# The order of the symmetry checks on VectorE: half comparisons spread between row comparisons, and W's loads behind the second row instead of the third

## The chip, the cores and the metric

The kernel runs on one core of one Trainium2 chip. The metric is the time of one execution on the device, in microseconds. It is in float32, and one launch computes everything.

## The reference

One FNet layer with a pre-norm is followed by one mixture-of-depths layer with a capacity of one token. The input `x` has 2048 tokens of 576 values.

```python
h  = x + FNet(layernorm(x))          # FNet: real part of a 2-D DFT
#   a = z @ dft_hid_re.T,  b = z @ dft_hid_im.T       (z = layernorm(x))
#   y = dft_seq_re @ a - dft_seq_im @ b               (2048 x 2048 matrices)
h2 = h + MoD(layernorm(h))
#   r = z2 @ w_r ; the token with the largest r goes through
#   (silu(z2 @ w_gate) * (z2 @ w_up)) @ w_down, times sigmoid(r)
#   (w_gate, w_up: 576 x 4608, w_down: 4608 x 576); all other tokens get nothing
```

All five matrices of the layers are inputs, so the DFT matrices too have to be read, and the kernel may not assume what they contain.

## The kernel before

**Folding.** A DFT matrix is symmetric under reversal of its index: the cosine is even, the sine odd. The kernel uses that to do only a part of the multiplications. Because the matrices are inputs, it also reads them from HBM in full and compares on the chip what it did not multiply with, against what it did. If any comparison differs, a flag (`miss`) decides at the end what is stored.

**Tiling.** Tokens are laid out as 128 partitions x 16 slots of 576 values (`X`). Column tiles of the sequence matrices are numbered j = 0..15, with part i = 0 (cosine) or 1 (sine); one such tile, "(j,i)", is 128 x 1152 float32 (576 KB by the profile's DMA issues) for the rows that are used, and a mirror part of 128 x 896 that is read only to be compared. The tiles come in two groups, `GROUPS = [[1,2,3,4,5],[6,7,0,8]]`. Those of group one (index 0 in the code) stay in the buffer `D` for the matmuls, their counterparts 16−j and all mirrors pass through the raw buffers `R` and through the free places of `D`.

**The comparisons.** There are two kinds.

- A row comparison, `c_check(j, i)`, makes three passes on VectorE: mirror of (j,i) against (j,i), mirror of (16−j,i) against (16−j,i) (both 896 wide, `off_s`, recorded as L418 or L420), and (16−j,i) against (j,i) (1152 wide, `off_t`, also L418 or L420). L418 is the form that also writes an accumulator. The call also loads what is missing: (16−j,i) on SP's queue (L394) and the mirrors by a gather on GpSimd's queue (L333).
- A half comparison, `c_half(g, c, m)`, compares the two halves of m tiles of `D`, in both parts, in passes of 128 x 5 x 64 and 128 x 4 x 64 per tile (`off_h`, L449 on VectorE; L423 is a short pause between two passes). For group one there are three: tiles 0–1, tiles 2–3, tile 4 (`HALVES[0] = [(0,2),(2,2),(4,1)]`). It loads nothing.

Each comparison writes its differences in bfloat16 to one of two slots of `Q`; ScalarE squares and sums them (L405), and the slot is free again after that. So each comparison waits for the square of the one two before it.

**W.** `w_first` issues the loads of the hidden-DFT matrix on SP's queue (L465 twice, 576 KB each, and a small one, L467), `wc_first` one gather of it on GpSimd's queue (L333 into `W`). W is needed by the hidden matmuls (L686) and by its own comparisons (`w_check`, `wc_check`).

**Queues.** SP issues plain loads in program order: a load whose buffer isn't free holds all loads behind it. GpSimd issues the gathers in its own program order, between its arithmetic. The profile lists the two as q1 and q0.

**The order.** A planner (`Plan.add`, `Plan.order`) gets all operations with an estimated duration and dependences, and lays out each engine's sequence. `Q` slots, raw buffers and the queues' order are assigned in the order in which the code calls the functions above, so the order of these calls sets which comparison comes after which, and which load is ahead of which. Between the comparisons VectorE also has the folds of the sequence results (`keep_step`, L659 into `Z`), the residuals (L695) and the router's dots (L699).

**The end.** The weights of the expert (L1330, L1338) are loaded by SP after the DFT matrices. VectorE, GpSimd (L1358) and ScalarE (L1363) form the products with the token, TensorE the last one (L1384); the last row is finished at L1395 and stored at L1405.

Of the kernel before, what the change touches and what calls it, by code (L numbers as in the profile page):

```python
# [37 lines left out]
GROUPS = [[1, 2, 3, 4, 5], [6, 7, 0, 8]]  # L38
# [5 lines left out]
HALVES = [[(0, 2), (2, 2), (4, 1)], [(0, 2), (2, 2)]]  # L44
# [31 lines left out]
class Plan:  # L76
# [6 lines left out]
    def add(self, eng, dur, fn, *deps, tail=0.0, push=0.0, holds=False, moves=False):  # L83
        flat = []
        for d in deps:
            flat += d if isinstance(d, list) else [d]
        n = {"eng": eng, "dur": dur, "fn": fn, "deps": [d for d in flat if d], "tail": tail, "push": push}
        n["holds"], n["moves"] = holds, moves
        n["i"] = len(self.ops)
        self.ops.append(n)  # L90
        return n
# [72 lines left out]
def kernel(  # L164
# [272 lines left out]
    def half_on_pool(g, c, i):  # L437
        return g == 1
# [343 lines left out]
    def then(f, *args):  # L782
        return lambda: f(*args)
# [41 lines left out]
    for a, b in X_RUNS:  # L825
# [4 lines left out]
        m = [add("ACT", 0.95, then(measure, k), f, push=push) for k, f in zip(ks, r)]  # L830
# [28 lines left out]
    for k in FOLDED:  # L859
        dg, use, at = [], [], []  # L860
        for sl in slots_of(k):
            n = next(places)
            UF[sl] = LATER[n]
            at.append(PLACE[n])
            if k in PAIRS:
                u, w = dgs.take()
# [42 lines left out]
    def c_load(j, i, mirror):  # L909
        CU[j, i, mirror] = ring("POOL" if mirror else "SP", load_c, 0.46 if mirror else 0.59, j, i, mirror)  # L910

    def c_first(g, i, cs=None):

        for c, j in enumerate(GROUPS[g]):
            if cs is not None and c not in cs:
                continue
            u = D_TAG[g, i], c
            if u in free:
                free.remove(u)
            w, users[u] = users[u], []  # L920
            LAST["SP"], d = load("SP", then(load_c, None, j, i, False), 0.59, w, LAST["SP"])
            CU[j, i, False] = u, d

    def c_half(g, c, m):
        u, w = qs.take()
        cus = [[CU[j, i, False] for j in GROUPS[g][c : c + m]] for i in range(2)]
        n = [
            add(
                *(("POOL", 0.3 + 1.31 * m) if half_on_pool(g, c, i) else ("DVE", 0.16 + 0.62 * m)),
                then(off_h, g, c, m, i, u), [d for _, d in cus[i]], w, PASSED if half_on_pool(g, c, i) else None,  # L930
                holds=not half_on_pool(g, c, i),
            )
            for i in range(2)
        ]
        for i in range(2):
            for b, _ in cus[i]:
                users[b].append(n[i])
        if (g, c + m) == (1, len(GROUPS[1])):
            HELD.append((u, 9 * m * P, n))
            return  # L940
        squares(u, 9 * m * P, n)
# [5 lines left out]
    def squares(u, w, n, ps=P, behind=None):  # L947
        SQUARES.append(add("ACT", 0.3 + w / 1200, then(square, u, w, ps), n, behind))
        qs.users[u].append(SQUARES[-1])

    def c_check(j, i):

        u, w = qs.take()
        u0, d0 = CU[j, i, False]
        c_load(j, i, True)
        u1, d1 = CU[j, i, True]
        n = [add("DVE", 1.08, then(off_s, j, i, u, 0), d0, d1, w, holds=True)]
        if (j, i) == GATE:
            PASSED.append(add("POOL", 0.1, lambda: pool.tensor_copy(gate[:, 1:2], gate[:, 0:1]), n))
        users[u0] += n  # L960
        users[u1] += n
        free.append(u1)
        if j in PAIRS:
            m = NK - j
            c_load(m, i, False)
            c_load(m, i, True)
            (u2, d2), (u3, d3) = CU[m, i, False], CU[m, i, True]
            n.append(add("DVE", 1.08, then(off_s, m, i, u, 1), d2, d3, w, holds=True))
            users[u3].append(n[1])
            n.append(add("DVE", 1.36, then(off_t, j, i, u), d0, d2, w, holds=True))  # L970
            users[u0].append(n[2])
            users[u2] += n[1:]
            free.extend([u3, u2])
        if u0[0] == "D1":
            free.append(u0)
        squares(u, QW if j in PAIRS else 7 * P, n)
# [3 lines left out]
    def w_first():  # L980
        for n in range(3):
            LAST["SP"], d = load(
                "SP", then(load_w, None, n), (0.59, 0.59, 0.005)[n], LAST["SP"], users["W" + "ABC"[n]]
            )
            WL.append(d)

    def wc_first():
        LAST["POOL"], d = load("POOL", then(load_w, None, 5), 0.295, LAST["POOL"])
        WC.append(d)

    def w_check():
        for n in range(2):
            u, d = ring("POOL", load_w, 0.59, n + 3)
            q, w = qs.take()
            o = add("DVE", 2.2, then(off_w, n, q), WL[n], d, w, holds=True)
            users[u].append(o)
            squares(q, 3 * D, o)
            WS.append(o)
            free.append(u)

    def wc_check():
        q, w = qs.take()
        WS.append(add("DVE", 2.6, then(off_wc, q), WL[2], WC, w))
        squares(q, D + 289, WS[-1])
# [91 lines left out]
        for b in [b for b in free if type(b) is tuple and b[0] == tag]:  # L1096
            free.remove(b)

    for c, m in HALVES[0]:
        c_half(0, c, m)  # L1100
    for n, j in enumerate(GROUPS[0]):
        if n == 3:
            w_first()
        if n == 3:
            wc_first()
        c_check(j, 0)
    for n in (0, 1, 4, 2, 3):
        seq_step(0, n)
        keep_step(0, n)
# [8 lines left out]
    no_more("D2")  # L1118
    free += [("D0", n) for n in range(N_D["D0"])]
    rows, first = iter(GROUPS[0]), iter(range(len(GROUPS[1])))  # L1120
    for step in "sffsffwcsss":
        if step == "s":
            c_check(next(rows), 1)
        elif step == "f":
            c_first(1, 0, (next(first),))
        elif step == "c":
            wc_check()
        else:
            w_check()
# [109 lines left out]
    step = add("DVE", 0.25, T["steps"][0], SCORES)  # L1239
    most = add("PE", 0.4, T["steps"][1], step)  # L1240
    step = add("DVE", 0.45, T["steps"][2], step)
    step = add("PE", 0.4, T["steps"][3], step, most)
    qx = add("DVE", 0.4, from_result, SCORES)
    rows = add("DVE", 0.55, T["steps"][4], most)
    slot = add("DVE", 1.1, token, step, rows)
    step = add("DVE", 1.0, where, slot, qx)
    step = add("ACT", 2.0, row_of_token, step, slot, RESULTS)
    squares(*HELD[0], behind=step)
    near = add("POOL", 1.0, other_rows, slot, push=50.0)
    step = add("PE", 1.2, to_all, step)  # L1250
# [33 lines left out]
    for b in range(NJ // TW):  # L1284
        j = TW * b
# [202 lines left out]
    with tc.If(T["mv"], preferred_fallthrough_block=False):  # L1488
        with ExitStack() as gen:
# [33 lines left out]
            with ExitStack() as hs:  # L1523
# [9 lines left out]
                with tc.For_i(0, NK, 1) as k:  # L1533
                    dve.tensor_copy(xr, row_of(GX, k))
                    norm(xn, xr, "x")
                    for a in range(5):
                        w = min(P, D - a * P)
# [4 lines left out]
                    for c in range(4):  # L1542
                        pa = zbank(f"gpa{c}")
                        for a in range(5):
                            w = min(P, D - a * P)
# [115 lines left out]
```

## Time and profile before

| | before |
|---|---|
| time, median of 3 runs | 197.28 us (195.94 to 198.41) |
| the profiled execution's own time | 197.32 us |
| its span | 195.3 us |
| mean granted TensorE clock | 0.86 |
| VectorE busy | 163.7 us (84%) |
| ScalarE busy | 140.4 us (72%) |
| TensorE busy | 130.8 us (67%) |
| GpSimd busy | 119.3 us (61%) |
| moved by DMA | 77.74 MB, mean 398 GB/s |

The span runs from the first to the last recorded instruction; the execution's own time is 2.0 us longer. Busy shares are means over stages: the checks and the DFT lie between 30 and 125 us, the router around 125 to 150 us, and the expert up to the end. A `DMA` row gives the mean busy share of the 16 DMA engines.

### The profile page before, as it was taken

The numbers are of one execution on the slowest core, as the hardware profiler recorded it, in microseconds if no ns is written. First come the engines' busy times: TensorE is split into PE (matmuls) and PEld (weight loads), VectorE is DVE, ScalarE is ACT, GpSimd is POOL, SyncE is SP. The second block draws the span as 40 slices with busy tenths as digits, with TensorE's granted clock in tenths as the row PEclk, the third lists the DMA queues.
The fourth block names the chain that finished last, engine by engine and source line by source line (L and its number), as shares of the span: only waits on it lengthen the run. The fifth ranks groups of instructions, "written<-read, shape, count | busy, mean of one in ns | idle before, by whom it ended". The sixth has DMA issues, their size and how long they took to land.

```text
span 195.3 us, 2824 instructions
## 1 busy us (share of the span) xinstructions
PE 130.8 (67%) x758; PEld 89.9 (46%) x758; DVE 163.7 (84%) x430; ACT 140.4 (72%) x260; POOL 119.3 (61%) x152
## 2 busy tenths in 40 slices
PE   0007999999999999999699989800241425073960
PEld 0005667765767788677576767500121212030340
DVE  2399999999899999997799999999739999979620
ACT  3298854782898697499289979697679898986600
POOL 6588888761515874076170006968639999999500
PEclk9999999999999999999999999985555555555599
DMA  5999999999999999999999999999999999999992
GB/s 182 414 413 411 412 411 406 411 403 396 408 410 411 413 404 406 408 413 411 407 403 392 422 428 393 422 410 368 425 426 425 416 433 425 421 419 416 411 425 92
DMA packets 14483, 77.74 MB, mean 398 GB/s; under 512 B 1911, under 2 KB 1915, under 8 KB 11134
## 3 DMA queue, kind: packets, MB, share of 16 engines
q1 hardware_dynamic: 10340, 56.34, 71.5%
q0 software_dynamic: 4112, 21.17, 26.8%
q8 instruction: 7, 0.11, 0.2%
q14 instruction: 14, 0.11, 0.2%
q10 hardware_dynamic: 10, 0.00, 0.0%
HBM read 72.78 MB, written 6.49 MB: 406 GB/s over the span
## 4 chain that ended last, share of the span: by engine, by line
DVE 31%; POOL 15%; issue 15%; DMA 11%; PE 5%; ACT 2%; ACTq 0%; SPq 0%; POOLq 0%; DVEq 0%
DVE Q L420 11%; POOL D L1358 8%; DMA R<-in_ct_dram 7%; DVE junk L699 6%; DMA D<-in_wt_dram,iw 4%; DVE X L695 4%; PE pd L1384 3%; DVE Z L659 2%; POOL R L1358 2%; DVE Q L418 2%; PE pk L1392 2%; POOL R L333 1%; POOL W L1358 1%; ACT Q L405 1%; POOL Q L1358 1%
## 5 line engine op out<-in xcount | busy, mean ns | idle before, releaser
L405 ACT ACTIVATE Q<-Q 128x2944 bf16<-128x2944 bf16 (+5 forms) x26 | 54.7, 2104 | 12.7 <-DVE Q L420 7.6
L686 PE MATMUL py<-W,Z 128*128 128x289 f32 x180 | 45.3, 409 | 1.0 <-DVE X L695 1.0
L641 PE MATMUL ps<-D,XF 128*128 128x320 f32 (+3 forms) x216 | 44.9, 407 | 1.6 <-DVE Z L659 1.6
L333 POOL DMA_INDIRECT R<-in_ct_dram,ic x22 | 24.7, 1121 | 27.3 <-DVE Q L420 15.9
L686 PEld LDWEIGHTS py<-W,Z 128*128 128x128 f32 x180 | 33.7, 189 | 12.3 <-PE py L686 1.8
L641 PEld LDWEIGHTS ps<-D,XF 128*128 128x128 f32 (+1 forms) x216 | 32.2, 172 | 13.8 <-issue 3.2
L1358 POOL TENSOR_TENSOR D<-D,Z 128x1152 f32<-128x1152 f32 x7 | 18.3, 2642 | 0.0
L574 ACT ACTIVATE junk<-X,XT 128x576 bf16<-128x576 f32 x16 | 12.3, 771 | 7.5 <-DVE W L535 6.3
L718 ACT ACTIVATE junk<-X,TD 128x576 bf16<-128x576 f32 x16 | 12.3, 768 | 5.4 <-DVE X L695 5.3
L420 DVE TENSOR_TENSOR Q<-D 128x896 bf16<-128x896 f32 (+1 forms) x13 | 15.0, 1186 | 1.0 <-ACT Q L405 1.0
L418 DVE SCALAR_TENSOR_TENSOR Q<-R,D 128x896 bf16<-128x896 f32 (+1 forms) x11 | 13.4, 1216 | 2.9 <-DMA R<-in_ct_dram 2.7
L420 DVE TENSOR_TENSOR Q<-R,D 128x896 bf16<-128x896 f32 (+1 forms) x13 | 15.0, 1163 | 0.0
L613 PE MATMUL fo<-W,diag 128*128 128x288 f32 (+1 forms) x8 | 4.2, 706 | 16.0 <-DVE diag L604 16.0
L333 POOL DMA_INDIRECT D<-in_ct_dram,ic x10 | 11.9, 1189 | 4.0 <-DVE Q L420 1.8
L699 DVE SCALAR_TENSOR_TENSOR junk<-X,wrz 128x576 bf16<-128x576 f32 x16 | 12.0, 752 | 0.4
L748 ACT ACTIVATE X<-X,BB,UP 128x576 f32<-128x576 f32 x14 | 10.9, 852 | 2.0 <-DVE BB L731 2.0
L695 DVE SCALAR_TENSOR_TENSOR X<-py,X 128x576 f32<-128x576 f32 x16 | 11.7, 753 | 0.0
L1384 PE MATMUL pd<-XF,H 128*1 128x144 f32 x80 | 5.1, 406 | 9.8 <-DVE H L1376 6.1
L1363 ACT ACTIVATE junk<-D 128x576 bf16<-128x576 f32 x16 | 10.9, 683 | 0.9 <-POOL D L1358 0.3
L1384 PE MATMUL pd<-D,H 128*1 128x144 f32 x128 | 7.5, 400 | 5.4 <-DVE H L1376 5.4
L447 POOL TENSOR_TENSOR Q<-D 128x640 bf16<-128x640 f32 (+1 forms) x8 | 11.0, 1400 | 0.0
L1347 DVE SCALAR_TENSOR_TENSOR junk<-R,xsp 128x576 bf16<-128x576 f32 x14 | 10.5, 751 | 0.3
(208 smaller groups left out, 264.9 us busy)
## 6 DMA issues: line engine op xcount, KB each, us to landing
D<-in_ct_dram SPq DMA_DIRECT2D x23, 576.0 KB
R<-in_ct_dram SPq DMA_DIRECT2D x9, 576.0 KB
D<-in_wu_dram SPq DMA_DIRECT2D x4, 1152.0 KB
D<-in_wd_dram SPq DMA_DIRECT2D x4, 1152.0 KB
R<-in_wg_dram SPq DMA_DIRECT2D x3, 1152.0 KB
D<-in_wg_dram SPq DMA_DIRECT2D x3, 1152.0 KB
R<-in_wu_dram SPq DMA_DIRECT2D x3, 1152.0 KB
out_dram<-X SPq DMA_DIRECT2D x2, 1440.0 KB
```

The lines of the kernel that those rows point to most:

```text
L333: pool.indirect_dma_start(tile, None, view, bass.IndirectOffsetOnAxis(ap=rows, axis=0), element_offset=at)
L405: act.activation(t, t, AF.Square, accum_out=DS[0 : t.shape[0], n : n + 1])
L418: dve.scalar_tensor_tensor(o, a, 1.0, b, op0=OP.mult, op1=op, accum_out=cell)
L420: dve.tensor_tensor(o, a, b, op=op)
L574: act.activation(junk[:, 0:D], X[:, k, 0:D], AF.Square, bias=XT[:, n : n + 1], scale=-float(D), accum_out=VX[:, n : n + 1],)
L641: pe.matmul(cm(ZP[g, n][k % 2][p0 : p0 + m], w), XF[:, q, m0 : m0 + m], DT[g, i][:, :, k, 0:HM], start=k in (0, 1), stop=k in (6, 7),)
L686: pe.matmul(YP[GROUPS[g][c]][:, h, 0:w], Z[:, a, c * P : (c + 1) * P], w_block(a)[:, h * HD : h * HD + w], start=(a == 0), stop=(a == 4),)
L695: dve.scalar_tensor_tensor(t, y, 1.0, t, op0=OP.mult, op1=OP.add, accum_out=TD[:, n, 1:2])
L699: dve.scalar_tensor_tensor(halves_of(junk2), halves_of(X[:, k, 0:D]), 1.0, YP["w"], op0=OP.mult, op1=OP.mult, accum_out=ON["dot"][:, n : n ...
L718: act.activation(junk[:, 0:D], X[:, k, 0:D], AF.Square, bias=TD[:, n, 1:2], scale=-float(D), accum_out=VAR[:, n : n + 1],)
L1358: pool.tensor_tensor(t, t, xs.unsqueeze(1).to_broadcast([P, JW, D]), op=OP.mult)
L1384: pe.matmul(T["pd"][at(h), :QD], H[:, j : j + 1], WB["d", j0][:, r, h * QD : (h + 1) * QD], start=(j == 0), stop=(j == NJ - 1),)
```

## The change

Before, the three half comparisons of group one are called first, then the rows 1 to 5 of part 0, with W's loads ahead of the fourth row. Now the calls follow the string `hrhrwrrr`: half comparison of tiles 0–1, row 1, half comparison of tiles 2–3, row 2, W's loads (plain and gathered), rows 3, 4 and 5. The third half comparison (tile 4) is called later, in the next string, behind row 1 of part 1 (`shffsffwcsss`).

```diff
-    for c, m in HALVES[0]:
-        c_half(0, c, m)
-    for n, j in enumerate(GROUPS[0]):
-        if n == 3:
+    pairs, rows = iter(HALVES[0]), iter(GROUPS[0])
+    for step in "hrhrwrrr":
+        if step == "h":
+            c_half(0, *next(pairs))
+        elif step == "w":
             w_first()
-        if n == 3:
             wc_first()
-        c_check(j, 0)
+        else:
+            c_check(next(rows), 0)
...
     rows, first = iter(GROUPS[0]), iter(range(len(GROUPS[1])))
-    for step in "sffsffwcsss":
-        if step == "s":
+    for step in "shffsffwcsss":
+        if step == "h":
+            c_half(0, *next(pairs))
+        elif step == "s":
             c_check(next(rows), 1)
         elif step == "f":
             c_first(1, 0, (next(first),))
```

Below the changed lines the line numbers grow by three (L1330 becomes L1333).

The first place is SP's queue, where the ten loads of group one's tiles into `D` end and the loads for the row comparisons into `R` begin; `W` is the hidden-DFT matrix. Before:

```order
L394 DMA D<-in_ct_dram 128x1152 x10
L394 DMA R<-in_ct_dram 128x1152 x3
L465 DMA W<-in_wt_dram 128x2x576 x2
L467 DMA W<-in_wt_dram 2x576
L394 DMA D<-in_ct_dram 128x1152
L394 DMA R<-in_ct_dram 128x1152 x2
L394 DMA D<-in_ct_dram 128x1152 x2
```

And now:

```order
L394 DMA D<-in_ct_dram 128x1152 x10
L394 DMA R<-in_ct_dram 128x1152 x2
L465 DMA W<-in_wt_dram 128x2x576 x2
L467 DMA W<-in_wt_dram 2x576
L394 DMA R<-in_ct_dram 128x1152
L394 DMA D<-in_ct_dram 128x1152
L394 DMA R<-in_ct_dram 128x1152 x2
```

The three loads into `R` are the tiles (15,0), (14,0) and (13,0), for the rows 1, 2 and 3. The third of them now stands behind W's three loads. On GpSimd's queue W's gather moves likewise, from behind two gathers of mirrors to ahead of them.

The second place is VectorE from the first row comparison on (`ps` and `os` are the sequence results that go to `Z`, `bt` belongs to the router). Before, from the first pass of row 1:

```order
L418 SCALAR_TENSOR_TENSOR Q,spill<-R,D 128x896
L418 SCALAR_TENSOR_TENSOR Q,spill<-R,D 128x1152
L420 TENSOR_TENSOR Q<-R 128x896
L659 SCALAR_TENSOR_TENSOR Z<-ps_0_395,os_0_425 128x5x64 x2
L449 TENSOR_TENSOR Q<-D 128x5x64
L423 SCALAR_TENSOR_TENSOR spill<-eps 128x1
L449 TENSOR_TENSOR Q<-D 128x4x64
L449 TENSOR_TENSOR Q<-D 128x5x64
L449 TENSOR_TENSOR Q<-D 128x4x64
L823 TENSOR_SCALAR bt<-tf 128x16
L420 TENSOR_TENSOR Q<-D,R 128x896
L420 TENSOR_TENSOR Q<-R,D 128x1152
```

And now, from the end of the second half comparison, row 1 being ahead of it, to the three passes of row 3:

```order
L449 TENSOR_TENSOR Q<-D 128x2x5x64
L449 TENSOR_TENSOR Q<-D 128x2x4x64
L823 TENSOR_SCALAR bt<-tf 128x16
L420 TENSOR_TENSOR Q<-R,D 128x896
L659 SCALAR_TENSOR_TENSOR Z<-ps_0_392,os_0_427 128x5x64 x2
L418 SCALAR_TENSOR_TENSOR Q,spill<-R,D 128x1152
L420 TENSOR_TENSOR Q<-R 128x896
L659 SCALAR_TENSOR_TENSOR Z<-ps_1_415,os_1_457 128x5x64 x2
L420 TENSOR_TENSOR Q<-R,D 128x1152
L420 TENSOR_TENSOR Q<-D,R 128x896
L420 TENSOR_TENSOR Q<-R,D 128x896
```

The half comparison of tile 4 no longer stands between rows 1 and 2. The rows 2 and 3 follow each other with only the first two folds into `Z` between them, and row 3 now begins with its 1152-wide pass, which reads the tile (13,0).

The third place is VectorE at the first two rows of part 1, ahead of the first residual (L695). Before:

```order
L659 SCALAR_TENSOR_TENSOR Z<-ps_3_492,os_3_522 128x5x64 x2
L418 SCALAR_TENSOR_TENSOR Q,spill<-R,D 128x1152
L418 SCALAR_TENSOR_TENSOR Q,spill<-R,D 128x896
L418 SCALAR_TENSOR_TENSOR Q,spill<-R 128x896
L418 SCALAR_TENSOR_TENSOR Q,spill<-R,D 128x1152
L418 SCALAR_TENSOR_TENSOR Q,spill<-R,D 128x896
L420 TENSOR_TENSOR Q<-R 128x896
L695 SCALAR_TENSOR_TENSOR X,TD<-py_0_532,X 128x576
```

And now:

```order
L420 TENSOR_TENSOR Q<-R 128x896
L659 SCALAR_TENSOR_TENSOR Z<-ps_3_491,os_3_523 128x5x64 x2
L449 TENSOR_TENSOR Q<-D 128x5x64
L423 SCALAR_TENSOR_TENSOR spill<-eps 128x1
L449 TENSOR_TENSOR Q<-D 128x4x64
L449 TENSOR_TENSOR Q<-D 128x5x64
L449 TENSOR_TENSOR Q<-D 128x4x64
L418 SCALAR_TENSOR_TENSOR Q,spill<-R,D 128x1152
L418 SCALAR_TENSOR_TENSOR Q,spill<-R,D 128x896
L420 TENSOR_TENSOR Q<-R 128x896
L695 SCALAR_TENSOR_TENSOR X,TD<-py_0_535,X 128x576
```

The half comparison of tile 4 (four passes and a pause) now stands between the rows 1 and 2 of part 1, and the last fold into `Z` stands between row 1 and it.

## The prediction

> **What bounds the kernel now.** I read the page's DMA rows first, then the chain of waits, then VectorE's timeline and the queues' rows in short windows. The page:
>
> ```profile
> GB/s 182 414 413 411 412 411 406 411 403 396 408 410 411 413 404 406 408 413 411 407 403 392 422 428 393 422 410 368 425 426 425 416 433 425 421 419 416 411 425 92
> DVE 31%; POOL 15%; issue 15%; DMA 11%; PE 5%; ACT 2%; ACTq 0%; SPq 0%; POOLq 0%; DVEq 0%
> ```
>
> The chain names VectorE first, with 31%, and the transfers with only 11%. But the transfer rate hardly falls in any slice. The table of windows (time in each engine, granted clock, then the share of the 16 DMA engines and GB/s) says how full they are:
>
> ```profile
> 5.00:40.00 35.00, 23.65 (x83) 16.97 (x84) 30.50 (x114) 23.80 (x51) 28.60 (x70) 1.00 1.02 411
> 40.00:80.00 40.00, 40.00 (x178) 28.91 (x177) 38.25 (x65) 29.22 (x38) 18.89 (x18) 1.00 1.02 407
> 80.00:86.00 6.00, 5.59 (x23) 4.08 (x22) 6.00 (x13) 4.87 (x7) 2.51 (x2) 1.00 1.01 406
> 86.00:115.00 29.00, 27.38 (x134) 20.64 (x133) 26.26 (x41) 22.94 (x35) 9.51 (x9) 1.00 1.01 409
> 115.00:150.00 35.00, 14.77 (x53) 10.28 (x51) 29.50 (x104) 28.53 (x47) 23.41 (x31) 0.72 1.01 411
> 150.00:190.00 40.00, 19.41 (x292) 9.04 (x292) 31.55 (x90) 29.53 (x83) 33.11 (x13) 0.56 1.01 421
> ```
>
> The DMA share is 1.01 or 1.02 in every stretch from 5 to 190 us. So the 16 DMA engines never lack work, and the kernel ends some microseconds after the last weights have come. The change moves no bytes away. A wait on VectorE is then worth something only if it decides when a load is issued late enough for the queues to run empty; and each microsecond in which they are empty is one at the end. No gain can come from filling them better.
>
> **What of VectorE's time the change can move.** Its timeline, with the wait ahead of an instruction in brackets:
>
> ```profile
> 41.08 0.48 DVE L449 TENSOR_TENSOR Q<-D 128x320 bf16<-128x320 f32 x1
> 42.63 0.17 DVE L823 TENSOR_SCALAR bt<-tf 128x16 f32<-128x16 f32 x1
> 43.24 1.09 DVE L420 TENSOR_TENSOR Q<-D,R 128x896 bf16<-128x896 f32 x1 [0.44 <-ACT Q L405]
> 46.52 0.88 DVE L659 SCALAR_TENSOR_TENSOR Z<-ps,os 128x320 f32<-128x320 f32 x2
> 47.32 1.34 DVE L420 TENSOR_TENSOR Q<-R,D 128x1152 bf16<-128x1152 f32 x1
> 52.55 3.36 DVE L420 TENSOR_TENSOR Q<-D 128x896 bf16<-128x896 f32 x3 [0.95 <-ACT Q L405]
> 59.89 0.88 DVE L659 SCALAR_TENSOR_TENSOR Z<-ps,os 128x320 f32<-128x320 f32 x2
> 60.69 1.35 DVE L418 SCALAR_TENSOR_TENSOR Q<-R,D 128x1152 bf16<-128x1152 f32 x1
> 64.41 1.41 DVE L418 SCALAR_TENSOR_TENSOR Q<-R,D 128x1152 bf16<-128x1152 f32 x1
> 67.88 0.75 DVE L695 SCALAR_TENSOR_TENSOR X<-py,X 128x576 f32<-128x576 f32 x1
> 76.97 3.36 DVE L420 TENSOR_TENSOR Q<-D 128x1152 bf16<-128x1152 f32 x3
> 94.11 1.36 DVE L418 SCALAR_TENSOR_TENSOR Q<-R,D 128x1152 bf16<-128x1152 f32 x1 [2.70 <-DMA R<-in_ct_dram]
> ```
>
> Two waits for ScalarE's squares stand here, 0.44 and 0.95 us, 1.39 together; with the half comparisons spread, both go. They are the most that the new order can save on VectorE.
>
> **W's loads ahead of row 3's.** Row 3 begins with a pass over (13,0), whose load is now behind W's. Up to and including it SP's queue carries the same bytes as before up to W's end. A tile has, by the page,
>
> ```profile
> D<-in_ct_dram SPq DMA_DIRECT2D x23, 576.0 KB
> ```
>
> which is 0.59 MB, half of W as much (128 x 1152 float32 too), and the nine slots of `X` that SP loads half of that each, 9 x 0.295: 2.65 + 10 x 0.59 + 3 x 0.59 + 2 x 0.59 = 11.5 MB. What q1, SP's queue, had moved from the start to 36, 46, 47 and 90 us, one answer each:
>
> ```profile
> q1 hardware_dynamic: 2448, 9.76, 69.6%
> q1 hardware_dynamic: 3085, 11.42, 63.9%
> q1 hardware_dynamic: 3132, 11.55, 63.3%
> q1 hardware_dynamic: 5436, 20.94, 59.1%
> ```
>
> 11.5 MB are through at 46.7 us. That is the lower bound for the landing of (13,0). A load lands later than the count of bytes says, since the 16 engines don't keep step: 20.94 MB is the sum up to the load of the chain's rows below (29 tiles, X and W), reached at 90.0, and that load landed at 80.74 + 13.28 = 94.0, which is 4.0 later. So the upper bound is 50.7 us; I take the middle, 48.7.
>
> When does VectorE ask? Rows 1 and 2 are done earlier now, since only half of the half comparisons stand ahead: before, `Z`'s second fold ended at 46.52 + 0.80 = 47.32. Now 1.55 us of the third half comparison (41.08 to 42.63) and the 0.44 wait are gone from before it, and about 0.9 us come in at row 1: its second pass reads (15,0) at about 35, where it read it at 38 before (bounds 0 and 3, by bytes near 1). So VectorE asks at about 46.2 and stands for 2.5 us, from 0.5 to 4.5, where before the load of (13,0) had come long before W.
>
> **From row 3 to the first residual.** Before, from 47.32 to 67.88, 20.56 us, 0.95 of them the wait. The new order does the same in between plus the half comparison of tile 4, 1.55 us: 21.15 us. Its second row of part 1 needs the slot of the first row, whose square ScalarE takes as that row ends:
>
> ```profile
> 64.35 2.66 ACT L405 ACTIVATE Q<-Q 128x2944 bf16<-128x2944 bf16 x1 [1.59 <-issue]
> 66.91 0.19 ACT L405 ACTIVATION_READ_ACCUMULATOR Q<-Q 128x1 f32 x1
> ```
>
> That is 2.85 us, and between the two rows VectorE has a fold (0.80) and the half comparison (1.55), 2.35: a wait of 0.5, or over 1 if ScalarE still makes the copy for that fold first; I take 0.7. The first residual then comes at 48.7 + 21.15 + 0.7 = 70.55, against 67.88: VectorE is 2.7 us late, from 0.7 (landing at 46.7) to 4.7 (50.7). The removed waits are in this sum.
>
> **Who waits for that.** The order on VectorE from there to the comparisons of row 3, part 1 (76.97, three passes) is the same as before. SP stands behind them, in the chain and in SP's own timeline:
>
> ```profile
> 79.25 1.09 DVE Q L420
> 80.36 0.33 SPq L394
> 80.74 13.28 DMA R<-in_ct_dram
> ```
>
> ```profile
> 72.81 7.87 SPq L394 DMA_DIRECT2D D<-in_ct_dram  x4
> ```
>
> One load goes at 73, the next three and the one into `R` only as these passes end, 79 to 81. What each queue moved in single microseconds, 81:82, then 82:83 (two rows), then 83:84 (two rows):
>
> ```profile
> q0 software_dynamic: 73, 0.41, 102.4%
> q0 software_dynamic: 45, 0.24, 61.6%
> q1 hardware_dynamic: 31, 0.14, 35.5%
> q1 hardware_dynamic: 84, 0.37, 91.0%
> q0 software_dynamic: 13, 0.05, 12.5%
> ```
>
> From 81 to 82 SP's queue moved nothing; GpSimd's gathers in q0 alone kept the engines full. At 82.0 they had 0.24 + 0.05 MB left and a little after, some 0.3 MB or 0.8 us at 0.41 MB/us, so they end at 82.8; SP's data come from about 82.3. The margin is 0.5 us. No gather can step in: GpSimd's next one waits for VectorE too. With VectorE 2.7 us late, SP's data come at 85.0, and the engines are empty from 82.8 to 85.0, for **2.2 us**. Bounds: 0.2 (late by 0.7) and 4.2 (by 4.7).
>
> From there VectorE's own lateness is no second cost: it had 2.70 us to stand at 91.4 for the load issued at 80.74. All later loads shift by the 2.2 us, with an engine share of 1.01 there is nothing in which to catch up, and the end follows.
>
> **The small terms.** W's gather ahead of two gathers of mirrors holds these up by about one gather,
>
> ```profile
> L333 POOL DMA_INDIRECT R<-in_ct_dram,ic x22 | 24.7, 1121 | 27.3 <-DVE Q L420 15.9
> ```
>
> 1.1 us; row 3 waits for (13,0) anyway: nothing. One pause less, 0.08 us, and one pass of row 1 in the cheaper form: in the 0.9 above, nothing. At the end the products have one row against a shift,
>
> ```profile
> 180.82 2.62 POOL L1358 TENSOR_TENSOR R<-R,Z 128x1152 f32<-128x1152 f32 x1 [0.33 <-SPq L1488]
> ```
>
> so GpSimd has 0.33 us to spare there, and the end takes the whole shift.
>
> The sum: 197.3 + 2.2 = **199.5 us**, on the profiled run's own 197.32 (span 195.3 and 2.0 around it), which is also the median, 197.28.
>
> **Two rules of the Trainium skill.** In 36 to 47 us the two queues shared the engines like this:
>
> ```profile
> q0 software_dynamic: 475, 2.61, 60.0%
> q1 hardware_dynamic: 684, 1.79, 42.8%
> ```
>
> The Trainium skill ("DMA: Bandwidth & Descriptors", section "Queues, rings and completion order") says that a DMA engine alternates between the queue rows that have work, a packet of each in turn. By an equal split of time, q1 would reach 11.5 MB about 1.5 us sooner (an estimate from that page and the rows), and the sum would be 198.0; the measured 42.8% decides here. What it says against the change holds either way: W's loads get no more than their turn, while the gathers run, and row 3's load stands behind them.
>
> **The rivals.**
>
> *The queues never run dry.* If (13,0) lands at 46.7, or loads released earlier by rows 1 and 2 leave more in the queues at 82 us, VectorE is late by less than the margin and the 2.70 us at 91.4 take the rest: **197.3**. For it: the full share everywhere. Against it: 0.5 us is a small margin.
>
> *The new order helps.* The 1.39 us of waits go, and loads are issued sooner. The transfers bound this: from 5 to 190 us there is no gap in their share to fill, so at most a few tenths at the ends, **196.9**.
>
> *A fuller queue moves more per microsecond.* As a mechanism: up to 115 us the engines move 409 GB/s with a share of 1.01, later up to 425 in single slices. If loads issued ahead brought the early part to 425, the 45 MB of 5 to 115 us (the first four rows of the windows, stretch by rate) would take 106 instead of 110 us: 197.3 − 4.1 = **193.2**. The rows speak against it: the share is full at either rate. The Trainium skill ("Perfetto Trace Analysis", section "Roofline") puts the ceiling of one core's 16 DMA engines at about 435 GB/s; the rows here stay below it, at 433 at most.
>
> *Slower by over 2%.* The same drought, longer: it is over the bound of 3.95 us once VectorE is over 4.45 us late at the passes of 76.97, which is so if (13,0) lands at 50.5 or later. At the upper bound 50.7 the engines stand for 4.2 us: **201.5**. For it: one load did land 4.0 us after its bytes' count. Against it: rows 1 and 2 free buffers earlier, and the load's lag was measured under a longer queue.
>
> **How the numbers follow.** Two per cent, 3.95 us, is about what a measurement of this kernel can tell from no change; faster is below 193.3, slower above 201.2. Chances: my forecast 0.50 (198.4 to 201.2), dry for longer 0.14, never dry 0.29, a small gain 0.05, the rate that rises 0.02. So faster 0.02, same 0.84, slower 0.14. The range runs from 196.7, which takes in the case without a drought, to 201.5, where the upper bound of the landing ends.
>
> **What would show it.** Right: on VectorE a wait of 1 to 4 us for `R<-in_ct_dram` ahead of a 1152-wide L420 at about 46 us; the brackets `<-ACT Q L405` of 0.44 and 0.95 gone; the first residual at 70 to 71 us; a slice between 80 and 90 us with a DMA share well below 1; the 2.70 us wait still there, or shorter, some 2 us later. Wrong: the first residual at 68.5 or earlier, or a full share from 5 to 190 us again; then the time is that of before. If the drought comes at 53 to 56 us, where row 3's late passes free their buffers, the mechanism is right and the place wrong. I would be wrong on the sign if the span came out below 195 us.

## The result and the profile after

The changed kernel takes 198.56 us (median of 20 runs, 197.51 to 200.43), the one before 196.45 us (median of 20, 195.71 to 198.41): a ratio of 1.0119, 95% interval 1.0098 to 1.0141. It is slower by 1.2%, clear of 1 by its interval, and by less than the 2% up to which the prediction calls the times the same. The forecast was 199.5 against 197.3, a ratio of 1.011. The size came out; the way there, as the trace shows, is another one. One profiled execution below, that of the kernel with fourteen more matmuls, was a disturbed one (204.47 us, that kernel's others 198.95 to 201.38), so that only durations are read from it and it is left out of the last table.

VectorE's timeline of the changed kernel at the places of the forecast:

```profile
46.12 1.36 DVE L420 TENSOR_TENSOR Q<-R,D 128x1152 bf16<-128x1152 f32 x1
64.44 1.36 DVE L418 SCALAR_TENSOR_TENSOR Q<-R,D 128x1152 bf16<-128x1152 f32 x1 [0.90 <-ACT Q L405]
67.87 0.75 DVE L695 SCALAR_TENSOR_TENSOR X<-py,X 128x576 f32<-128x576 f32 x1
76.96 3.36 DVE L420 TENSOR_TENSOR Q<-D 128x1152 bf16<-128x1152 f32 x3
94.46 1.36 DVE L418 SCALAR_TENSOR_TENSOR Q<-R,D 128x1152 bf16<-128x1152 f32 x1 [3.06 <-DMA R<-in_ct_dram]
```

Row 3's pass at 46.12 has no wait in brackets. The first residual comes at 67.87, before at 67.88, and the passes that SP waits for at 76.96, before at 76.97. VectorE is not late at all there, and so the queues don't run dry. The windows:

```profile
80.00:86.00 6.00, 6.00 (x26) 4.63 (x26) 5.96 (x13) 4.87 (x7) 2.65 (x2) 1.00 1.01 405
115.00:150.00 35.00, 20.60 (x68) 14.64 (x66) 25.98 (x94) 25.81 (x44) 20.21 (x29) 0.74 1.00 398
```

The share from 80 to 86 us is 1.01 as before. In the stretch from 115 to 150 us TensorE is busy for 20.6 us instead of 14.8, and VectorE for 26.0 instead of 29.5. There the time goes. The chain of waits of the changed kernel goes through it: VectorE's residuals (L695) at 112.79, TensorE's hidden matmuls (L686) from 114.20, and a residual at 132.15.

TensorE's timeline, first before, then after (L686 are the hidden-DFT matmuls, 20 records for each tile):

```profile
105.38 10.32 PE L686 MATMUL py<-W,Z 128*128 128x289 f32 x40
116.28 9.99 PE L686 MATMUL py<-W,Z 128*128 128x289 f32 x40 [0.58 <-DVE X L695]
```

```profile
105.73 5.14 PE L686 MATMUL py<-W,Z 128*128 128x289 f32 x20
114.20 17.91 PE L686 MATMUL py<-W,Z 128*128 128x289 f32 x60 [3.32 <-DVE X L695]
```

Before, TensorE waits 0.58 us between the four tiles of group two and is done at 126.3. After, it waits 3.32 us behind the first of them, for residuals on VectorE, and then needs 17.91 us for 60 records, 299 ns each instead of 250; it is done at 132.1. The windows (last three columns: granted clock, engine share, GB/s) say why they are slower; of before, then of after:

```profile
114.00:118.00 4.00, 3.42 (x14) 2.40 (x14) 3.96 (x10) 3.19 (x3) 0.00 (x0) 1.00 1.02 429
```

```profile
114.00:117.00 3.00, 2.80 (x6) 2.08 (x7) 3.00 (x8) 3.00 (x5) 0.10 (x1) 0.50 1.04 436
117.00:120.00 3.00, 3.00 (x7) 2.12 (x7) 2.07 (x6) 2.90 (x9) 3.00 (x4) 0.50 0.95 384
120.00:123.00 3.00, 3.00 (x13) 2.26 (x12) 0.61 (x1) 1.15 (x4) 3.00 (x3) 0.94 1.03 414
```

Behind the wait the granted clock is 0.50 for over six microseconds. Why TensorE waits is in VectorE's order at 100 to 118 us. Before, the residuals of py4 (the last tile of group one, whose matmuls are over by 92 us) come one pass behind the last fold; after, the three passes of a row comparison stand between. Before, then after:

```order
L659 SCALAR_TENSOR_TENSOR Z<-ps_4_737,sgn,os_4_769 128x4x64 x2
L420 TENSOR_TENSOR Q<-D 128x896
L695 SCALAR_TENSOR_TENSOR X,TD<-py_4_672,X 128x576 x2
```

```order
L659 SCALAR_TENSOR_TENSOR Z<-ps_4_735,sgn,os_4_764 128x4x64 x2
L420 TENSOR_TENSOR Q<-R,D 128x1152
L420 TENSOR_TENSOR Q<-R,D 128x896
L420 TENSOR_TENSOR Q<-R 128x896
L695 SCALAR_TENSOR_TENSOR X,TD<-py_4_670,X 128x576 x2
L420 TENSOR_TENSOR Q<-D 128x896
L695 SCALAR_TENSOR_TENSOR X,TD<-py_0_777,X 128x576
L418 SCALAR_TENSOR_TENSOR Q,gate<-R,D 128x896
L695 SCALAR_TENSOR_TENSOR X,TD<-py_0_777,X 128x576
```

These residuals free the PSUM tile into which TensorE writes its next tile. They end at 114.1 instead of 110.5 us: the fold comes 1.4 us later, and three passes take 2.3 us more than one. The planner sorts this stretch anew, although nothing in it was edited, presumably because a half comparison that moves changes the times by which it picks. Besides, the gate pass (L418 into `gate`) now stands between the two residuals of py0.

VectorE in its turn stands for TensorE's late results, 3.29 us here and not at all before, where it has no wait in brackets from 116 to 138 us. After:

```profile
122.39 0.76 DVE L695 SCALAR_TENSOR_TENSOR X<-py,X 128x576 f32<-128x576 f32 x1 [3.29 <-PE py L686]
```

The way to the end is the token: after the hidden matmuls the router finds it (`cit`), GpSimd forms its products with the expert's weights, and the last row follows (`orow`). Before, then after:

```profile
140.09 0.15 DVE L319 TENSOR_SCALAR cit<-gt 128x1 int32<-128x1 f32 x1
146.80 2.62 POOL L1358 TENSOR_TENSOR XF<-XF,Z 128x1152 f32<-128x1152 f32 x1 [2.82 <-ACT Z L1228]
189.99 0.37 DVE L1395 SCALAR_TENSOR_TENSOR orow<-pd,sg,orow 97x144 f32<-97x144 f32 x1 [2.31 <-PE pd L1384]
```

```profile
144.54 0.15 DVE L319 TENSOR_SCALAR cit<-gt 128x1 int32<-128x1 f32 x1
151.32 2.62 POOL L1361 TENSOR_TENSOR XF<-XF,Z 128x1152 f32<-128x1152 f32 x1 [2.89 <-ACT Z L1231]
184.94 2.62 POOL L1361 TENSOR_TENSOR R<-R,Z 128x1152 f32<-128x1152 f32 x1
194.08 0.37 DVE L1398 SCALAR_TENSOR_TENSOR orow<-pd,sg,orow 97x144 f32<-97x144 f32 x1 [2.31 <-PE pd L1387]
```

The token comes 4.45 us later, GpSimd's fourteen products start 4.5 us later and follow each other without a gap, and the last row is 4.1 us later. The span grows by 3.1 us in these two executions. It ends 5.3 us behind the last row before and 4.3 us behind it after: before, SP's queue, which stores other rows, still moves 0.10 MB behind 191.7 us, when the store of the last row has been issued; after, it moves nothing behind that point (195.8 us).

### The profile page after: what moved, and what is told of

It is laid out like the page before. It is cut to its first block, busy times and chain, and to the rows that moved or that the text cites. A ratio compares the mean times of both kernels' runs of the same rounds, so it can differ in the third digit from the quotient of the medians.

```text
span 198.4 us, 2828 instructions
## 1 busy us (share of the span) xinstructions
PE 133.3 (67%) x758; PEld 92.4 (47%) x758; DVE 163.9 (83%) x429; ACT 140.5 (71%) x260; POOL 124.9 (63%) x152
## 4 chain that ended last, share of the span: by engine, by line
DMA 29%; DVE 24%; PE 14%; issue 13%; POOL 13%; ACT 4%; SPq 0%; DVEq 0%; POOLq 0%; ACTq 0%
DMA R<-in_ct_dram 15%; DVE Q L420 9%; PE py L686 9%; DMA D<-in_ct_dram 8%; POOL D L1361 6%; DMA R<-in_ct_dram,ic 5%; DVE junk L699 3%; PE pd L1387 3%; ACT Q L405 3%; DVE X L695 2%; POOL R L1361 2%; DMA X<-in_x_dram 2%; DVE Z L659 2%; PE pk L1395 1%; POOL W L1361 1%
## 5 line engine op out<-in xcount | busy, mean ns | idle before, releaser
L686 PE MATMUL py<-W,Z 128*128 128x289 f32 x180 | 47.9, 427 | 3.3 <-DVE X L695 3.3
L641 PE MATMUL ps<-D,XF 128*128 128x320 f32 (+3 forms) x216 | 45.2, 408 | 1.9 <-DVE Q L420 1.8
L686 PEld LDWEIGHTS py<-W,Z 128*128 128x128 f32 x180 | 35.7, 200 | 15.1 <-DVE X L695 3.8
L333 POOL DMA_INDIRECT R<-in_ct_dram,ic x22 | 27.4, 1246 | 21.8 <-DVE Q L420 9.8
L641 PEld LDWEIGHTS ps<-D,XF 128*128 128x128 f32 (+1 forms) x216 | 32.7, 172 | 14.0 <-issue 3.5
L418 DVE SCALAR_TENSOR_TENSOR Q<-R,D 128x1152 bf16<-128x1152 f32 (+1 forms) x12 | 14.7, 1221 | 4.5 <-DMA R<-in_ct_dram 3.5
L695 DVE SCALAR_TENSOR_TENSOR X<-py,X 128x576 f32<-128x576 f32 x16 | 11.6, 751 | 3.7 <-PE py L686 3.5
L333 POOL DMA_INDIRECT D<-in_ct_dram,ic x10 | 12.4, 1243 | 3.5 <-issue 2.1
L420 DVE TENSOR_TENSOR Q<-R,D 128x896 bf16<-128x896 f32 (+1 forms) x12 | 13.7, 1150 | 0.1
L1366 ACT ACTIVATE junk<-D 128x576 bf16<-128x576 f32 x18 | 12.3, 683 | 1.1 <-POOL D L1361 0.5
L1387 PE MATMUL pd<-D,H 128*1 128x144 f32 x160 | 8.6, 377 | 6.6 <-DVE H L1379 5.5
L1387 PEld LDWEIGHTS pd<-XF,H 128*1 128x1 f32 x80 | 2.2, 108 | 18.8 <-DVE H L1379 12.6
```

The lines of the kernel that those rows point to most:

```text
L333: pool.indirect_dma_start(tile, None, view, bass.IndirectOffsetOnAxis(ap=rows, axis=0), element_offset=at)
L418: dve.scalar_tensor_tensor(o, a, 1.0, b, op0=OP.mult, op1=op, accum_out=cell)
L420: dve.tensor_tensor(o, a, b, op=op)
L641: pe.matmul(cm(ZP[g, n][k % 2][p0 : p0 + m], w), XF[:, q, m0 : m0 + m], DT[g, i][:, :, k, 0:HM], start=k in (0, 1), stop=k in (6, 7),)
L686: pe.matmul(YP[GROUPS[g][c]][:, h, 0:w], Z[:, a, c * P : (c + 1) * P], w_block(a)[:, h * HD : h * HD + w], start=(a == 0), stop=(a == 4),)
L695: dve.scalar_tensor_tensor(t, y, 1.0, t, op0=OP.mult, op1=OP.add, accum_out=TD[:, n, 1:2])
```

## The experiments

The theory: the planner's new order puts py4's residuals behind three passes; TensorE waits for them, its clock falls, the token is late, and the end is the token plus some 49.6 us. Its rivals: W's loads (the forecast's mechanism), the spread of the half comparisons by itself, and the other order of the expert's loads, which also differs between the two kernels.

### The halves alone and W alone

```diff
-    for step in "hrhrwrrr":            # the change
+    for step in "hrhrrwrr":            # halves alone: W ahead of the fourth row, as before
```

```diff
-    for step in "hrhrwrrr":            # the change
+    for step in "hhhrrwrrr":           # W alone: the three half comparisons first, as before
...
-    for step in "shffsffwcsss":
+    for step in "sffsffwcsss":
```

> Only the half comparisons spread; W's loads stay ahead of the fourth row, as before. If the late residuals of the fifth hidden tile (py4) cause the loss, nothing of it goes: VectorE's order at 100 to 118 us is that of the changed kernel, TensorE should wait about 3.3 us for L695 at about 111 us and then run at a granted clock of 0.50 for some us, ratio to before 1.008 to 1.016. If W's loads ahead of row 3's load cause it, the ratio is 0.998 to 1.003.

> Only W's loads moved behind the second row; the three half comparisons stand first, as before. By the late residuals: VectorE's order at 100 to 118 us is that of before, TensorE waits 0.6 us there, no drop of the clock before 128 us, ratio 0.998 to 1.003. By W's loads: ratio 1.008 or more.

The halves alone: ratio 1.0116 (1.0054 to 1.0177), the whole loss. TensorE:

```profile
114.46 16.45 PE L686 MATMUL py<-W,Z 128*128 128x289 f32 x60 [3.32 <-DVE X L695]
```

W alone: ratio 1.0044 (1.0008 to 1.0080), neither of the two numbers expected. TensorE has no such wait at this place. VectorE is even 0.9 us early at the passes that SP waits for (76.09), and yet a load costs time, though not row 3's. VectorE's timeline, then TensorE's:

```profile
95.44 1.36 DVE L418 SCALAR_TENSOR_TENSOR Q<-R,D 128x1152 bf16<-128x1152 f32 x1 [4.91 <-DMA R<-in_ct_dram]
```

```profile
98.63 7.69 PE L641 MATMUL ps<-D,XF 128*128 128x256 f32 x34 [2.62 <-DVE Z L659]
```

The load into `R` that before costs a wait of 2.70 us, until 94.11, now costs 4.91, until 95.44, though it was issued 0.9 us earlier. TensorE waits for a fold behind that pass, 2.62 us where before it was 1.58, and here too the granted clock falls behind the wait, to 0.50 from 99.7 to 103.1 us. The hidden matmuls start at 108.40 instead of 105.38: 1.3 us by the load and, as an estimate from half a rate over 3.4 us, 1.7 by the clock. The token is 1.8 us later (141.87). Why this load takes longer wasn't tried. In the whole change its wait is 3.06 us, TensorE's wait behind it 1.83 us, and the clock stays at 1.00:

```profile
97.64 8.16 PE L641 MATMUL ps<-D,XF 128*128 128x256 f32 x54 [1.83 <-DVE Q L420]
```

The whole change loses no more than the halves alone.

### The residuals, moved by hand

The next two move py4's residuals in the planner's finished order and leave all else: once in the changed kernel, ahead of the three passes; once in the kernel before, the other way.

```diff
     todo = plan_ffn(best[1])[1]
+    for r in RESID[0, 4][::-1]:                        # py4's two residuals
+        todo.remove(r)
+        todo.insert(todo.index(KEPT[1][4]) + 1, r)     # right behind the last fold
     apart = plan.apart(todo)
```

> The changed kernel with one edit behind the planner: the two residuals of py4 stand ahead of the three row-comparison passes that they follow in the changed kernel; all else, the expert's loads and products included, keeps the changed kernel's order. By the late residuals: no wait of TensorE over 1 us at 105 to 125 us, clock 1.00 there, last hidden matmul at about 126 us instead of 132, ratio 0.995 to 1.004. If the changed order of the expert's loads or the spread of the half comparisons itself costs the time, the ratio stays at 1.008 to 1.016.

> The kernel before with the opposite edit alone: py4's two residuals stand behind the four passes that follow them. No half comparison and no load is moved. By the late residuals: TensorE waits about 4.4 us at about 110 us, its clock falls to 0.50 for some 7 us, the last hidden matmul ends 6 to 7 us later, and the ratio is 1.010 to 1.020. If the spread or the loads cause the loss, the ratio is 0.998 to 1.003.

In the kernel before, the late residuals alone cost 2.8%: ratio 1.0281 (1.0233 to 1.0330), more than the change and above my 1.010 to 1.020. TensorE waits 4.46 us, the clock falls, the token comes at 146.05 and the last row at 195.05. No load and no half comparison was moved. The cause is strong enough. TensorE's timeline:

```profile
115.17 17.67 PE L686 MATMUL py<-W,Z 128*128 128x289 f32 x60 [4.46 <-DVE X L695]
```

The windows show the clock behind it:

```profile
114.00:118.00 4.00, 2.83 (x6) 2.10 (x7) 3.97 (x12) 3.46 (x6) 0.00 (x0) 0.50 1.01 419
```

But in the changed kernel the early residuals helped nothing: 1.0123 (1.0066 to 1.0180), against my 0.995 to 1.004. The wait had only moved by one tile (the timelines of TensorE and of VectorE):

```profile
118.68 11.67 PE L686 MATMUL py<-W,Z 128*128 128x289 f32 x40 [2.88 <-DVE X L695]
116.75 1.09 DVE L418 SCALAR_TENSOR_TENSOR Q<-R,D 128x896 bf16<-128x896 f32 x1 [1.20 <-ACT Q L405]
```

The windows behind it:

```profile
119.00:122.00 3.00, 3.00 (x8) 2.13 (x7) 2.97 (x9) 2.94 (x8) 3.00 (x3) 0.50 1.01 402
```

The gate pass waits 1.20 us for ScalarE's square, the second residual of py0 stands behind it, and TensorE waits for that one, 2.88 us; the clock falls again. So the new order holds two late residuals in a row, and mending the first uncovers the second. The next kernel mends both:

```diff
+    todo.remove(gates[0])                              # the gate pass
+    todo.insert(todo.index(RESID[1, 0][1]) + 1, gates[0])   # behind py0's second residual
```

> The changed kernel with two edits behind the planner: py4's two residuals ahead of the three passes, and the gate pass (L418 into gate) behind the second residual of the second group's first tile (py0) instead of between its two. Theory (the end is the finding of the token plus some 49.6 us of products): no wait of TensorE over 1 us at 105 to 125 us, last hidden matmul at 126 to 128 us, token found (cit) at 140 to 141.5 us, ratio 0.998 to 1.005. Rival (the spread of the half comparisons or the order of the expert's loads costs the time by itself): TensorE doesn't wait, and the ratio is 1.010 all the same.

Ratio 1.0013 (0.9988 to 1.0037): the loss is gone, with the half comparisons spread, W's loads moved and the expert's loads in the changed order. So none of the three rivals costs the changed kernel time, 0.4% at most by the interval. The token and the last row:

```profile
139.92 0.15 DVE L319 TENSOR_SCALAR cit<-gt 128x1 int32<-128x1 f32 x1
190.04 0.37 DVE L1400 SCALAR_TENSOR_TENSOR orow<-pd,sg,orow 97x144 f32<-97x144 f32 x1 [2.31 <-PE pd L1389]
```

The planner finds such an order by itself if one letter moves, the third half comparison to behind row 2:

```diff
-    for step in "hrhrwrrr":
+    for step in "hrhrhwrrr":
...
-    for step in "shffsffwcsss":
+    for step in "sffsffwcsss":
```

> The change with one letter moved: the third half comparison (tile 4) stands behind row 2, ahead of W's loads, instead of behind row 1 of part 1. Spread of the first two and W's loads as in the changed kernel; the planner then puts py4's residuals ahead of the last fold and the gate pass behind both residuals of py0. Theory: no wait of TensorE over 1 us at 105 to 125 us, token found at 139 to 141.5 us, ratio 0.997 to 1.005. Rival (the spread or W's loads): 1.008 or more.

Ratio 1.0001 (0.9979 to 1.0022). TensorE waits 0.31 us at this place, and the token comes at 139.95.

### The clock behind the wait

Is it the wait that costs, or what it does to the clock? Here TensorE gets matmuls to do in the wait, whose result nobody uses. The residuals stay late.

```diff
+    def filler():
+        t = zpair("fill")[0]
+        for _ in range(14):                            # then: 6
+            pe.matmul(t[:, 0:HD], Z[:, 0, 0:P], w_block(0)[:, 0:HD], start=True, stop=True)
+    todo.insert(todo.index(HIDS[1, 0]) + 1, ...)       # behind the first tile of group two
```

> The changed kernel with 14 matmuls more (128x128 by 128x288, result not used) on TensorE between the first and the second hidden tile of group two, that is, in its wait of 3.3 us. The wait for the residuals stays, the engine isn't idle in it. If the drop of the granted clock to 0.50 behind the wait costs part of the time: clock 1.00 from 114 to 125 us, the 60 matmuls behind the wait take 15 us instead of 17.9, token found 2.5 to 3 us earlier than in the changed kernel (at about 142), ratio 1.003 to 1.008. If the clock falls for another reason than the idle time, or doesn't matter: clock 0.50 there as before, ratio 1.009 to 1.015.

> The changed kernel with 6 filling matmuls instead of 14 in TensorE's wait. Fourteen took 6.95 us, since each is two passes of 0.25 us, and ran 3 us past the wait; six take 3.0 us and fit in it. Idle time lowers the clock: clock 1.00 from 111 to 125 us, the 60 matmuls behind the wait in 14.8 us instead of 17.9, token found 2.5 to 3.1 us earlier than in the changed kernel, ratio to before 1.002 to 1.008. If the clock didn't matter, the ratio stays at that of the changed kernel, run beside it.

> The changed kernel itself, beside the filled one on the same chip: ratio 1.009 to 1.015, TensorE's wait of 3.3 us at 111 us, clock 0.50 behind it for about 7 us, token found at 144 to 145 us.

Fourteen were too many. Ratio 1.0179 (1.0137 to 1.0221), since a float32 matmul is two records of 0.25 us and they ran past the wait: the filling took 6.95 us, but the 60 records behind it 14.79 instead of 17.91.

```profile
113.81 6.95 PE L1487 MATMUL fill<-W,Z 128*128 128x288 f32 x28
120.60 14.79 PE L686 MATMUL py<-W,Z 128*128 128x289 f32 x60
```

Six fit. TensorE's timeline with six, then the windows, and then the windows of the changed kernel run beside it:

```profile
109.67 3.07 PE L1487 MATMUL fill<-W,Z 128*128 128x288 f32 x12
113.16 14.90 PE L686 MATMUL py<-W,Z 128*128 128x289 f32 x60 [0.41 <-DVE X L695]
```

```profile
114.00:118.00 4.00, 4.00 (x18) 3.12 (x17) 3.97 (x11) 3.94 (x10) 2.14 (x3) 1.00 1.04 433
```

```profile
114.00:117.00 3.00, 3.00 (x8) 2.07 (x7) 3.00 (x8) 2.97 (x7) 0.64 (x2) 0.50 1.04 433
117.00:120.00 3.00, 3.00 (x13) 2.35 (x12) 1.53 (x4) 2.94 (x8) 3.00 (x3) 0.94 1.00 418
```

With six, the ratio is 1.0015 (0.9985 to 1.0044); the changed kernel beside it has 1.0114 (1.0079 to 1.0149). The residuals still come late (they end at 113.1 us, in the changed kernel beside it at 113.6, before at 110.5), the clock stays at 1.00, and nearly the whole loss is gone. The 60 records take 14.90 us instead of 16.58 in the run beside it. That is 1.7 of the 2.2 us by which the token comes earlier (140.48, 142.67); the other 0.5 are the earlier residuals. So what costs is mostly the clock behind the wait. The wait by itself costs little here because VectorE has other work: the hidden matmuls end 1.8 us later than before (128.06, 126.27), the token only 0.4 us (140.48, 140.09).

### The forecast's mechanism by itself

The forecast said that a VectorE that is late lets the queues run dry. That can be tried without the change: four passes of 128x576 more on VectorE, at 43 us, in the kernel before.

```diff
+    def idle_work():
+        for _ in range(4):
+            dve.tensor_tensor(junk2, X[:, 0, :], X[:, 1, :], op=OP.add)
+    todo.insert(min(todo.index(n) for n in CHK[3, 0]), ...)   # ahead of the second row comparison
```

> The kernel before with four more passes of 128x576 on VectorE (0.67 us each, 2.7 us together, result not used) at about 43 us, ahead of the second row comparison. The prediction's mechanism: VectorE is 2.2 us late at the passes of 76.97 us, SP's loads come 2.2 us later, the queues are empty for some 1.7 us at 83 to 85 us, and the time grows by as much, ratio 1.007 to 1.011. Rival: the lateness is taken up by the wait of 2.70 us at 91 to 94 us and by what the queues still hold, engine share 1.00 at 80 to 90 us, ratio 0.998 to 1.003.

Ratio 1.0098 (1.0069 to 1.0128), as the mechanism asks; but not at its place. The windows, then VectorE's timeline:

```profile
50.00:52.00 2.00, 1.13 (x3) 0.77 (x4) 2.00 (x4) 0.00 (x0) 0.94 (x1) 0.75 0.66 234
52.00:54.00 2.00, 2.00 (x5) 1.30 (x4) 2.00 (x3) 0.92 (x1) 0.74 (x1) 0.50 0.53 203
80.00:88.00 8.00, 8.00 (x35) 6.30 (x34) 7.94 (x15) 4.00 (x8) 0.88 (x1) 1.00 1.01 405
```

```profile
81.12 3.36 DVE L420 TENSOR_TENSOR Q<-D 128x1152 bf16<-128x1152 f32 x3
```

The engines run dry from 50 to 54 us, near the place that the prediction names for a drought (53 to 56 us), and 0.34 x 2 + 0.47 x 2 = 1.6 us of them are missing there. They are full at 80 to 88 us, although the passes there are over 4 us late; presumably the transfers are then late themselves. TensorE also waits 2.72 us there (to 50.87), its clock is at 0.50 from 51.0 to 54.4, and the token is 1.4 us later. But at the end GpSimd's last product waits 0.95 us for its load, where before it was 0.33, and the span ends 5.3 us behind the last row as before, so that here the transfers seem to set the end. How much of the loss is theirs and how much the clock's, this run doesn't separate. So a late VectorE can let the queues run dry; in the changed kernel it isn't late there, and they don't.

### Token and end in the profiled executions

| kernel | token found, us | last row, us | between | ratio |
|---|---|---|---|---|
| before | 140.09 | 189.99 | 49.9 | 1 |
| changed, py4's residuals early and the gate pass behind py0's | 139.92 | 190.04 | 50.1 | 1.0013 |
| third half comparison behind row 2 | 139.95 | 190.14 | 50.2 | 1.0001 |
| six matmuls in the wait | 140.48 | 189.84 | 49.4 | 1.0015 |
| VectorE late at 43 us | 141.48 | 192.38 | 50.9 | 1.0098 |
| W alone | 141.87 | 191.18 | 49.3 | 1.0044 |
| changed, run again | 142.67 | 193.32 | 50.7 | 1.0114 |
| changed, py4's residuals early | 142.78 | 192.51 | 49.7 | 1.0123 |
| halves alone | 143.33 | 193.78 | 50.5 | 1.0116 |
| changed | 144.54 | 194.08 | 49.5 | 1.0119 |
| before, py4's residuals late | 146.05 | 195.05 | 49.0 | 1.0281 |

Token and last row are of one execution each, the ratio of 6 to 20. From token to last row it is 49.0 to 50.9 us in every kernel. No run finds the token more than 0.2 us earlier than before's, so what an earlier token would be worth is not shown.

## Why the prediction was right in size and wrong in its reason

**What bounds the kernel: half right.** Before, the transfers are full from 5 to 190 us and end behind the last row, and nothing was gained, as said. But the statement that a wait counts only if it empties a queue is wrong. A second path is nearly as long: the token and the products behind it. With both residuals early that path starts at 139.92 and GpSimd's products run without a gap to the same end; before, they have one gap of 0.33 us. The two bounds are about a microsecond apart (5.3 us from the last row to the end of the span before, 4.3 after), and the change lengthened the one that the forecast had left out. I had the row with the 0.33 us, and read it as slack for the transfers to use up instead of as the sign of a second bound.

**W's loads ahead of row 3's: the term failed.** I put the landing of (13,0) at 48.7 us, between 46.7 and 50.7, and the wait at 2.5 us. The pass ran at 46.12 without a wait, below the lower bound. That bound assumed that SP's queue would move its bytes at before's rate, and this is the first step that failed. What the queues moved after (packets, MB, share of the engines), first from 36 to 45 us, then SP's queue from the start to 44 us:

```profile
q1 hardware_dynamic: 727, 1.99, 58.0%
q0 software_dynamic: 305, 1.66, 46.2%
```

```profile
q1 hardware_dynamic: 3154, 11.59, 67.5%
```

11.5 MB were through at about 43.5, not 46.7: q1 had 58.0% of the engines, where before it had 44.9% from 36 to 45 us, and q0 less. The other end of the range was as unsound: the pass ran 2.6 us behind the count of bytes, so that the load's lag was no more than that, not 4.0. An equal split, which I had weighed and set aside for before's 42.8%, gave 45.2 and was nearer.

**From row 3 to the first residual: right in its terms.** The wait for the square in the last place was 0.90 us (0.7 taken), the one at row 1, for the load of (15,0), 0.40 (0.9 taken), and the old waits of 0.44 and 0.95 are gone. With row 3's wait left out, my sum would have been within half a microsecond of 67.87.

**Who waits for that: the step that failed most.** I followed VectorE's order only as far as 77 us, wrote that it is the same as before up to there, and took all behind it as shifted by one number. The order that decides lies at 100 to 118 us, and could be read before the run: three passes ahead of py4's residuals, the gate pass between py0's. What the profile of before had of it is the state without the loss: TensorE's clock at 1.00 up to 130 us, with waits of no more than 0.58 us between its hidden tiles. It has no row for the price of a longer one; the changed kernel's 3.32 us and 17.91 instead of some 15 us for 60 records are that price.

**The rivals.** "The queues never run dry" was true, with 197.3 as its price wrong. "The new order helps" and "a fuller queue moves more" didn't happen. (The last one's price was misread: behind 115 us the page's slices reach 433 GB/s, not 425, which would have given some 191 us.) That the planner would sort another stretch anew was no rival of mine. By the prediction's own signs it failed: the first residual came at 67.87, ahead of 68.5, and the share from 80 to 86 us was full. The drought of 2.2 us didn't come, and a loss of about the same size came from a path that the sum doesn't contain. That 199.5 fits is luck.

## What to carry to other kernels

Where a planner sets the order, read the new order to the end, above all at the places where the engine on the longest path waits, even if the edit is 60 us ahead of it. Where transfers are full from start to end, still look for a second path that is as long, by taking a run's fixed distances from its end (here 49 to 51 us from the token). A wait on TensorE costs itself and what it does to the clock; six matmuls without use in it cost hardly more here than a better order (1.0015 against 1.0001 and 1.0013).

## What the hardware showed that I had not expected

Up to 125 us, a wait of TensorE between its matmuls of 2.62, 2.72, 2.88, 3.32 or 4.46 us was followed by a granted clock of 0.50; one of 1.83 us or less wasn't. The clock fell 2.6 to 3.7 us after the wait began, in some kernels only when TensorE was at work again. It then stayed at 0.50 for 3.4 or 6.8 us, and for no length between, although TensorE worked: for 6.8 us where TensorE came back 0.7 us (the changed kernel's first profile, 113.5 to 120.3) or 1.2 us (before with late residuals) after the fall, and for 3.4 us where it came back ahead of the fall or 0.2 us behind it (the changed kernel run again, 113.9 to 117.3, the halves alone, W alone, py4's residuals early, VectorE late). The changed kernel's wait was 3.32 us both times, and its token differed by 1.9 us (144.54, 142.67).

The Trainium skill ("TensorE: Matmul & The Clock Gate", section "Part 1: The HAM clock gate (the "warmup" mystery)") has the clock at half its rate after an idle window of about 3.4 us, and at the full rate again after about 3.4 us of work. The traces agree in kind; here 2.62 us were enough to lower it, and the clock stayed low for 3.4 us or twice that. The Trainium skill, in the same section, calls the window free-running, so that the moment of return depends on where work begins in it. The two lengths above fit that; no run here set the moment on purpose.

And a load's landing isn't told by the bytes ahead of it alone: SP's queue went from 45 to 58% of the engines, from 36 to 45 us, though in the two queues' lists only W's loads stand in another place (the passes that free their buffers moved too). What sets the shares wasn't tried.
